# Two stores per token tile issued by ScalarE in place of SyncE, in a two-layer fp32 kernel

## The chip, the cores and the metric

The kernel runs on one core of a Trainium2 chip. The metric is the device time of one execution in microseconds, the median of several runs. Before the change it is 719.97 us (3 runs, 719.19 to 720.18).

## The reference

What is computed is two rounds of the same pair of residual blocks on x of 2048 tokens by 576 features:

```python
x = x + _A_ref(_layernorm(x), A_wqkv, A_wo)          # linear attention, 32 heads of 18
x = x + _B_ref(_layernorm(x), B_w_q, B_k1, B_k2, B_u, B_v)   # product-key experts, top 1 per head
```

Block A projects to q, k and v, applies phi(t) = elu(t) + 1 + 1e-6 to q and k, sums k times v over all tokens into one state per head, and divides q times state by q times the sum of k. Block B scores 64 experts per head, takes the best one, and adds gelu(x . u[e]) v[e].

## The kernel before

The 2048 tokens are 16 tiles of 128. A tile passes through named pieces of code, each a Python generator that is run up to its next `yield`. `front_T` (`fT`) turns the normalized tile so that features lie on partitions, and splits it into two float32r operands: `thif`, written by ScalarE (line 117), and `tlof`, the remainder, written by VectorE (line 118). `front_k`, `front_v` and `front_q` multiply them by the weights on TensorE (`ppk`, `ppv`, `ppq`, line 258); `front_state` adds the tile into the state (`kva`). For the second half of layer A, `num` divides (`o`), `oT` turns `o` into `thio` and `tloo`, `O` multiplies by the folded output weights (`ppo`, line 483) and adds the residual on VectorE (`x`, line 473). Block B is `bT`/`S` (scores, `kva` or `pps`, line 525), `gel`, `sel` (ten small VectorE operations that end in `cg`, line 590), `cT` (`ptc`, `chi`, `clo`) and `po` (line 609, residual again line 473).

A layer norm after a residual is a relay: VectorE's `x` with its sum, POOL's `mb` or `mf` (line 187), ScalarE's `junk` with a squared sum (line 188), three POOL instructions (`rsb` or `rsf`, 193 to 195), and ScalarE's `yb` or `yf` (line 205).

Most tiles of layer 0's second half and of layer 1's front are not turned on TensorE but by VectorE and memory (`moved`): VectorE transposes 32 by 32 squares (`ro`, `rb`, `rf`, line 229), one DMA stores 320 KB (`y_do`, `y_db`, `y_df`, line 231), and four DMAs of 80 KB load it back (`go`, `gb`, `gf`, line 237). The next reader is ScalarE's split at line 117.

Layer 1's q is not computed in the front. For tiles 0 to 12, `front_keep` (lines 330 to 334) stores `thif` and `tlof` of layer 1, 320 KB each, to `hl_d`; `late_load` (lines 340 and 341) loads them when the state is complete, from 499 us on.

The order of the work is written out by hand, in strings that `play` reads: `keep1.5` stands for `front_keep` of layer 1, tile 5. Within `in_order(*ALL)` the instructions of TensorE, ScalarE, VectorE and POOL stand exactly in that order. SyncE is not among them: its queue, which issues every DMA before the change, is ordered by the framework's scheduler. The middle part of the program (about 290 to 435 us) is one string of two tiles played four times, with other pieces before and after it. The framework gives the DMAs eight completion semaphores in turn; a DMA waits until the last DMA with its semaphore has landed.

```python
with in_order(*ALL):
    for s in range(5, 13, 2):
        play("""bT0.0 num0.2 ... ld0.3 k1.-3 O0.1 ... keep1.-2 v1.-2 po0.-1 ... keep1.-1 st1.-2 ...""", s)
```

Of the kernel before, what the change touches and what calls it, by code (L numbers as in the profile page):

```python
# [11 lines left out]
F32 = mybir.dt.float32  # L12
# [52 lines left out]
def network(ctx, tc, x_in, wqkv, wo, wq_t, k_t, u_t, v2, c_mask, c_mask4, c_ident, c_code, c_code1, c_scale, c_shift, out):  # L65
    nc = tc.nc
# [44 lines left out]
    hl_d = [dr.tile([P, 2, NB, P], F32, name=f"hl_d{t}") for t in range(NT)]  # L111
# [218 lines left out]
    def front_keep(l, t):  # L330

        hi, lo = tt["f", l, t]
        nc.sync.dma_start(hl_d[t][:, 0], hi.bitcast(F32))
        nc.sync.dma_start(hl_d[t][:, 1], lo.bitcast(F32))

    def late_load(l, t):

# [405 lines left out]

    bc = object()
    keep, rl, lq, ldx, ldq = front_keep, late_load, late_q, back_x, back_pq
    fl, ln, lv, sv = first_load, first_ln, load_vu, split_vu
    k, v, q, fT, st = front_k, front_v, front_q, front_T, front_state
# [210 lines left out]
```

## Time and profile before

| | |
|---|---|
| median of 3 runs | 719.97 us |
| the profiled execution, its own time | 720.89 us |
| its span (first to last instruction) | 719.1 us |
| mean granted TensorE clock | 0.997 |
| TensorE, VectorE, ScalarE, POOL busy | 698.8, 474.0, 320.9, 202.7 us |
| DMA bytes | 107 MB, all by SyncE's queue but for instruction loads |

Times in the views are microseconds from the start of the span. A row of the timeline has start, duration, engine (SPq is SyncE's queue, PEld TensorE's weight load), line, operation, tiles, shapes and count; in brackets stands the idle time of the engine just before, and what ended it. Rows of equal instructions are merged. Tile numbers are left out there; they follow from the order.

### The profile page before, as it was taken

Reading aid. Unit: us, or ns where it says so; the run is one execution under the profiler, and the core shown is the slowest. Engines: PE = TensorE matmul, PEld = TensorE weight load, DVE = VectorE, ACT = ScalarE, POOL = GpSimd, SP = SyncE. Lnnn points to the kernel's source line nnn. Section 1 sums busy time; section 2 is a strip of 40 time slices with the busy share of each in tenths; the row PEclk is TensorE's granted clock in tenths of the full one; section 3 lists DMA queues with packets and bytes.
Section 4 is the critical chain, followed back from the end, with each engine's and each line's share of the span. In section 5 each row is a group of like instructions: output and inputs, shape, how many; then the busy total and the mean of one; then the engine's idle time right before and its main releaser. Section 6 shows DMA issues by size and latency. Waiting matters only on the chain. (4 is left out here: it accounts for less than half of the span.)

```text
span 719.1 us, 14715 instructions
## 1 busy us (share of the span) xinstructions
PE 698.8 (97%) x5464; PEld 649.9 (90%) x5464; DVE 474.0 (66%) x1031; ACT 320.9 (45%) x658; POOL 202.7 (28%) x543
## 2 busy tenths in 40 slices
PE   8999999999999999999999999999999999999995
PEld 6999989999998999899898989899899999899984
DVE  5533343435437877687787878552647798988996
ACT  4522422342224456455555554644543534444443
POOL 2211000111004533344343433210323244433431
PEclk9999999999999999999999999999999999999998
DMA  8847777774312322476767665423632324111101
GB/s 252 274 159 249 262 237 260 253 216 137 112 33 67 100 103 102 147 232 199 238 219 234 205 198 172 138 61 121 170 106 83 112 71 134 51 67 51 51 17 66
DMA packets 82711, 107.17 MB, mean 149 GB/s; under 512 B 8976, under 2 KB 47376, under 8 KB 82640
## 3 DMA queue, kind: packets, MB, share of 16 engines
q1 hardware_dynamic: 82640, 106.24, 46.7%
q8 instruction: 43, 0.70, 0.4%
q14 instruction: 28, 0.23, 0.1%
HBM read 68.88 MB, written 37.32 MB: 148 GB/s over the span
## 5 line engine op out<-in xcount | busy, mean ns | idle before, releaser
L483 PE MATMUL ppo<-ohi,thio 126*128 126x252 f32 (+1 forms) x320 | 50.6, 300 | 3.9 <-ACT thio L117 3.9
L483 PEld LDWEIGHTS ppo<-ohi,thio 126*128 126x128 f32 (+1 forms) x320 | 44.9, 189 | 5.8 <-ACT thio L117 4.9
L188 ACT ACTIVATE junk<-x,mb 128x576 bf16<-128x576 f32 x32 | 24.8, 775 | 49.0 <-POOL mb L187 43.0
L205 ACT ACTIVATE yb<-x,rsb 128x640 f32<-128x640 f32 x32 | 29.5, 921 | 35.7 <-POOL rsb L195 35.7
L258 PE MATMUL ppk<-whi,thif 128*128 128x252 f32 (+1 forms) x300 | 45.2, 297 | 0.1
L258 PE MATMUL ppv<-whi,thif 128*128 128x252 f32 (+1 forms) x300 | 44.7, 295 | 0.1
L179 POOL TENSOR_SCALAR rsf<-mvf 128x1 f32<-128x1 f32 x16 | 3.4, 211 | 146.9 <-DVE mvf L176 146.8
L453 POOL TENSOR_TENSOR o<-pq,zb 128x576 f32<-128x576 f32 x19 | 27.3, 1439 | 60.9 <-ACT zb L399 57.4
L258 PE MATMUL ppv<-whi,tlof 128*128 128x252 f32 (+1 forms) x300 | 43.9, 293 | 0.0
L258 PE MATMUL ppk<-whi,tlof 128*128 128x252 f32 (+1 forms) x300 | 43.9, 293 | 0.0
L258 PEld LDWEIGHTS ppk<-whi,thif 128*128 128x128 f32 x300 | 40.9, 188 | 3.1 <-issue 2.9
L258 PEld LDWEIGHTS ppv<-whi,thif 128*128 128x128 f32 x300 | 41.3, 188 | 1.1 <-issue 0.4
L258 PEld LDWEIGHTS ppk<-whi,tlof 128*128 128x128 f32 x300 | 41.2, 188 | 0.0
L258 PEld LDWEIGHTS ppv<-whi,tlof 128*128 128x128 f32 x300 | 41.2, 188 | 0.0
L483 PE MATMUL ppo<-olo,thio 126*128 126x252 f32 (+1 forms) x256 | 39.6, 293 | 0.0
L258 PE MATMUL ppq<-whi 128*128 128x252 f32 (+1 forms) x260 | 39.5, 299 | 0.0
L483 PE MATMUL ppo<-ohi,tloo 126*128 126x252 f32 (+1 forms) x256 | 39.5, 293 | 0.0
L277 DVE TENSOR_SCALAR ek<-ek 128x576 f32<-128x576 f32 x16 | 7.4, 460 | 46.2 <-ACT ek L276 46.2
L258 PEld LDWEIGHTS ppq<-whi 128*128 128x128 f32 x260 | 36.0, 189 | 0.6 <-DVE eq L287 0.3
L483 PEld LDWEIGHTS ppo<-olo,thio 126*128 126x128 f32 x256 | 36.2, 188 | 0.0
L258 PE MATMUL ppk<-wlo,thif 128*128 128x252 f32 x240 | 36.1, 293 | 0.0
L258 PE MATMUL ppv<-wlo,thif 128*128 128x252 f32 x240 | 36.1, 293 | 0.0
(205 smaller groups left out, 1781.5 us busy)
## 6 DMA issues: line engine op xcount, KB each, us to landing
fold<-in_wq_t SPq DMA_DIRECT2D x64, 288.0 KB, 4.2
whi<-hl_d SPq DMA_DIRECT2D x26, 320.0 KB, 4.4
y_df<-rf SPq DMA_DIRECT2D x23, 320.0 KB, 3.0
gf<-y_df SPq DMA_DIRECT2D x92, 80.0 KB, 2.1
pq_d<-eq SPq DMA_DIRECT2D x19, 288.0 KB, 2.2
pq<-pq_d SPq DMA_DIRECT2D x19, 288.0 KB
xf<-in_x SPq DMA_DIRECT2D x16, 288.0 KB, 2.7
x<-in_x SPq DMA_DIRECT2D x16, 288.0 KB, 2.7
```

Source lines behind the costliest of these rows:

```text
L179: nc.gpsimd.tensor_scalar(rs[:, 0:1], mv[:, 1:2], EPS_LN, 1.0, op0=ALU.add, op1=ALU.mult)
L188: nc.scalar.activation(junk, xt, AF.Square, bias=m[:, 0:1], accum_out=m[:, 1:2])
L205: nc.scalar.activation(y, x2, AF.Identity, scale=rs[:, 0:1], bias=rs[:, 1:2])
L258: nc.tensor.matmul(o[:, at:at + c1 - c0], tt[a == "lo"][:, b, :], wb[:, cols + c0:cols + c1], start=(i == 0), stop=(i == len(todo) - 1))
L277: nc.vector.tensor_scalar(e, e, 1.0, EPS, op0=ALU.min, op1=ALU.add)
L453: nc.gpsimd.tensor_tensor(o[:, :D], pq, zb, op=ALU.mult)
L483: nc.tensor.matmul(p[:, at:at + c1 - c0], hl[a][:r, b], w[:r, c0:c1], start=(i == 0), stop=(i == len(todo) - 1))
```

## The change

The two stores of `front_keep` are issued by ScalarE's queue. With that they become ScalarE instructions, and `in_order` holds them at their place in the string.

```diff
     def front_keep(l, t):
 
         hi, lo = tt["f", l, t]
-        nc.sync.dma_start(hl_d[t][:, 0], hi.bitcast(F32))
-        nc.sync.dma_start(hl_d[t][:, 1], lo.bitcast(F32))
+        nc.scalar.dma_start(hl_d[t][:, 0], hi.bitcast(F32))
+        nc.scalar.dma_start(hl_d[t][:, 1], lo.bitcast(F32))
```

TensorE's and VectorE's rows stay as they were; ScalarE has 26 rows more and SyncE 26 fewer.

ScalarE, at tile 4 of layer 1 (the first of the even tiles 4, 6, 8, 10 of the repeated string). `hl_d_92` is tile 4's store, `thif_4` the operand just split, `junk,mb_7` the layer norm of tile 7 of layer 0:

```order
 L117 ACTIVATE thib_6_4135<-gb_6_4130 128x640
 L117 ACTIVATE thif_4_4157<-gf_4_4152 128x640
+L333 DMA hl_d_92<-thif_4_4157 128x640
+L334 DMA hl_d_92<-tlof_4_4158 128x640
 L188 ACTIVATE junk,mb_7_4244<-x_7_4209,mb_7_4244 128x576
 L117 ACTIVATE chi_5_4165<-ptc_5_4163 128x128
```

Both stores now stand between the split of `thif_4` and the square sum of tile 7; the second waits for VectorE's `tlof_4`.

ScalarE, at tile 5 (the odd tiles 3, 5, 7, 9), where `yf_6` is the end of another layer norm:

```order
 L205 ACTIVATE yb_8_4498<-x_8_4461,rsb_8_4494 128x640
 L188 ACTIVATE junk,mf_6_4500<-x_6_4489,mf_6_4500 128x576
+L333 DMA hl_d_93<-thif_5_4469 128x640
+L334 DMA hl_d_93<-tlof_5_4470 128x640
 L205 ACTIVATE yf_6_4538<-x_6_4489,rsf_6_4534 128x640
 L539 ACTIVATE g_7_4547<-s_7_4459 128x64
```

Here they stand between a square sum and the normalization that waits for POOL.

SyncE's queue at the same place, with `go_9` the four loads behind `y_do_9`:

```order
 L231 DMA y_do_9_4473<-ro_9_4471 128x640
-L333 DMA hl_d_93<-thif_5_4469 128x640
-L334 DMA hl_d_93<-tlof_5_4470 128x640
 L237 DMA go_9_4607<-y_do_9_4473 32x4x160
 L617 DMA x_d_142<-x_6_4489 128x576
-L237 DMA go_9_4607<-y_do_9_4473 32x4x160
+L237 DMA go_9_4607<-y_do_9_4473 32x4x160 x3
 L231 DMA y_db_8_4595<-rb_8_4593 128x640
-L237 DMA go_9_4607<-y_do_9_4473 32x4x160 x2
 L231 DMA y_df_6_4620<-rf_6_4618 128x640
```

The stores are gone, and the last two of the four loads stand ahead of `y_db_8` instead of behind it.

## Prediction

> **What bounds the kernel now.** I read the page first, then TensorE's timeline of the stretch that holds the stores, then the waits of that stretch, and from there back along the engines that TensorE waited for.
>
> ```profile
> PE 698.8 (97%) x5464; PEld 649.9 (90%) x5464; DVE 474.0 (66%) x1031; ACT 320.9 (45%) x658; POOL 202.7 (28%) x543
> L334 SPq DMA_DIRECT2D hl_d<-tlof x13: 319/320/434, 263.8 to 456.5; - x13
> ```
>
> TensorE is busy for 97% of the span, so a change that leaves it alone can save at most its 20 us of idle time, and costs only where it makes TensorE wait. The second store of each tile (from the rows of `hl_d`: count, duration min/median/max in ns, first and last start) comes between 263.8 and 456.5 us. TensorE's timeline there has few gaps:
>
> ```profile
> 350.41 0.33 PE L512 MATMUL ptc<-ident,cg 128*128 128x128 f32 x1
> 351.57 1.59 PE L483 MATMUL ppo<-ohi,thio 126*128 126x252 f32 x10 [0.83 <-ACT thio L117]
> 384.33 1.59 PE L483 MATMUL ppo<-ohi,thio 126*128 126x252 f32 x10 [0.89 <-ACT thio L117]
> 417.05 1.59 PE L483 MATMUL ppo<-ohi,thio 126*128 126x252 f32 x10 [0.83 <-ACT thio L117]
> 437.70 0.51 PE L609 MATMUL po<-vmix,chi 128*128 128x252 f32 x2 [0.87 <-DVE ek L287]
> ```
>
> The repeated string takes 32.7 us for two tiles, and in each turn TensorE waits 0.83 to 0.89 us for ScalarE's `thio` of the odd tile. So each turn is bound by a loop through the other engines, not by TensorE. Its last links are these, of SyncE's queue and of ScalarE:
>
> ```profile
> 340.70 0.32 SPq L231 DMA_DIRECT2D y_do<-ro  x1
> 341.75 0.32 SPq L333 DMA_DIRECT2D hl_d<-thif  x1
> 342.61 0.32 SPq L334 DMA_DIRECT2D hl_d<-tlof  x1
> 344.24 0.32 SPq L237 DMA_DIRECT2D go<-y_do  x1
> 344.65 0.41 SPq L617 DMA_DIRECT2D x_d<-x  x1
> 345.11 0.42 SPq L237 DMA_DIRECT2D go<-y_do  x1
> 345.69 0.34 SPq L231 DMA_DIRECT2D y_db<-rb  x1
> 346.08 2.00 SPq L237 DMA_DIRECT2D go<-y_do  x2
> 350.78 0.74 ACT L117 ACTIVATE thio<-go 128x640 fp32r<-128x640 f32 x1 [2.38 <-DMA go<-y_do]
> ```
>
> ScalarE idles 2.38 us for the last `go`. The first `go` waits for the landing of `y_do`, not for the stores of `hl_d`; the last two stand behind `y_db`, whose data VectorE has only just made.
>
> **The stores on the even tiles: a wait in ScalarE.** The loop's earlier links, ScalarE first, then VectorE:
>
> ```profile
> 323.05 0.74 ACT L117 ACTIVATE thif<-gf 128x640 fp32r<-128x640 f32 x1 [1.45 <-DMA gf<-y_df]
> 324.43 0.78 ACT L188 ACTIVATE junk<-x,mb 128x576 bf16<-128x576 f32 x1 [0.63 <-POOL mb L187]
> 324.26 0.82 DVE L118 TENSOR_TENSOR tlof<-gf,thif 128x640 fp32r<-128x640 f32 x1
> 327.46 0.85 DVE L229 STREAM_TRANSPOSE rb<-yb 128x640 f32<-128x640 f32 x1 [1.68 <-ACT yb L205]
> 336.70 0.76 DVE L287 SCALAR_TENSOR_TENSOR ek<-ek,ppk 128x576 f32<-128x576 f32 x1 [0.38 <-ACT ek L286]
> 349.98 0.29 DVE L590 TENSOR_TENSOR cg<-g,c 128x128 f32<-128x128 f32 x1
> ```
>
> Before, `junk` starts at 324.43. Now it stands behind the second store, which waits until `tlof` is written at 324.26 + 0.82 = 325.08. The first store's issue fits ahead of that. How soon a store follows its `tlof`, SyncE showed a tile earlier:
>
> ```profile
> 310.23 0.82 DVE L118 TENSOR_TENSOR tlof<-gf,thif 128x640 fp32r<-128x640 f32 x1 [0.91 <-ACT thif L117]
> 311.08 0.32 SPq L334 DMA_DIRECT2D hl_d<-tlof  x1
> ```
>
> `tlof` ends at 311.05 and the issue starts 0.03 us later; by the row of line 334 an issue takes 0.32 to 0.43 us. No row shows a DMA issued by ScalarE; its cost lies between nothing and SyncE's longest issue of these tiles, 1.49 us:
>
> ```profile
> L237 SPq DMA_DIRECT2D go<-y_do x32: 318/444/1487, 312.3 to 424.9; - x32
> ```
>
> I take 0.38, the middle of the store's own rows. So `junk` moves by 0.65 + 0.03 + 0.38 = **1.06 us**, and with it everything queued behind: `chi`, POOL's `rsb`, `yb`, and VectorE's `rb`, which waited for `yb` already. VectorE then runs without a gap until `ek` at 336.70, whose 0.38 us wait takes up that much. From there the shift is 1.06 - 0.38 = 0.68 us, at `ro` (and so `y_do`) and at `cg`.
>
> Two chains then end at the same TensorE rows. By `cg`: 349.98 + 0.29 + 0.68 = 350.95, so `ptc` moves from 350.41 to 350.95 and `ppo` could start 0.33 later, at 351.3; that is 0.26 us earlier than 351.57, if `thio` is there. By `go`: 0.68 us later than 351.57, less what SyncE's shorter queue gives.
>
> **What SyncE's shorter queue gives.** The last two `go` no longer wait for `y_db`: with 0.43 us each behind the second they start at 345.54 and 345.97 (before, 346.08 and about 0.5 later), so some 0.55 us sooner. They also no longer lie behind the 320 KB of `y_db`. At the best rate of the stretch from 300 to 440 us (40 slices of it), 338 GB/s, that is 0.95 us:
>
> ```profile
> GB/s 241 135 207 332 237 197 236 313 240 120 133 164 333 245 173 173 273 338 124 143 168 321 266 153 160 262 301 209 167 96 260 298 260 107 181 297 251 101 129 99
> ```
>
> Against this stand the stores themselves. Before they moved at 342 to 345 us, while `go` had to wait for `y_do` anyway. Now ScalarE issues them behind `junk` of `mf`:
>
> ```profile
> 344.79 0.19 ACT L188 ACTIVATION_READ_ACCUMULATOR junk<-x,mf 128x1 f32 x1
> 346.19 0.92 ACT L205 ACTIVATE yf<-x,rsf 128x640 f32<-128x640 f32 x1 [1.21 <-POOL rsf L195]
> ```
>
> The two issues, 0.76 us, fit in the 1.21 us in which `yf` waits for POOL, so ScalarE loses nothing on odd tiles. But 640 KB, 1.9 us at 338 GB/s, now run beside the very loads that TensorE waits for. The gain is 0.55 + 0.95 less 0 to 1.9, that is -0.4 to 1.5 us; I take 0.3, near the low end, because the stores start within a microsecond of the loads. The Trainium skill (DMA: Bandwidth & Descriptors, section "Issuing engines are not separate DMA queues") says that DMAs of all engines interleave on the same 16 DMA engines, and that issuing from another engine saves only the sequencer's time; by it the gain would be the 0.55 alone less the sharing. The trace of before has one queue and can't show it.
>
> So a turn changes by 0.68 - 0.3 = **+0.4 us**, with ends of -0.26 (the `cg` chain) and +1.1. There are three such turns (351.57, 384.33, 417.05): **+1.2 us**. The turn before them has no even store behind it yet, and I count nothing.
>
> **The last even tile.** Tile 10's stores stand at 422.6, and its loop ends elsewhere, at TensorE's 437.70:
>
> ```profile
> 422.45 0.82 DVE L118 TENSOR_TENSOR tlof<-gf,thif 128x640 fp32r<-128x640 f32 x1
> 422.61 0.78 ACT L188 ACTIVATE junk<-x,mb 128x576 bf16<-128x576 f32 x1 [0.59 <-POOL mb L187]
> 425.65 0.85 DVE L229 STREAM_TRANSPOSE rb<-yb 128x640 f32<-128x640 f32 x1 [1.68 <-ACT yb L205]
> 435.74 0.35 DVE L460 RECIPROCAL r<-den 128x32 f32<-128x32 f32 x1 [0.41 <-POOL den L457]
> 437.47 0.28 DVE L118 TENSOR_TENSOR clo<-ptc,chi 128x128 fp32r<-128x128 f32 x1
> ```
>
> The shift is 423.27 + 0.03 + 0.38 - 422.61 = 1.07 us. VectorE has no gap between 425.65 and `clo` but the 0.41 us for POOL's `den`, which follows VectorE's own and moves along. TensorE, which waited 0.87 us here, waits **1.07 us** more.
>
> **The other stores.** Tile 11's stores stand late in the string, between the third folded weight and the second late q:
>
> ```profile
> 514.97 0.65 ACT L423 ACTIVATE ohi<-m 126x576 fp32r<-126x576 f32 x1
> 515.95 0.65 ACT L284 ACTIVATE eq<-ppq 128x576 f32<-128x576 f32 x1 [0.33 <-PE ppq L258]
> 518.58 1.35 PEld L258 LDWEIGHTS ppq<-whi 128*128 128x128 f32 x10 [0.30 <-DVE eq L287]
> ```
>
> 0.76 us of issue less the 0.33 us of idle delay `eq`, on whose end the next `ppq` waits already: **+0.43 us** (0 to 2.6). Tile 0's stores stand ahead of `junk` at 278.74, those of tiles 1 and 2 ahead of 292.91, tile 12's ahead of 458.18:
>
> ```profile
> 278.74 0.78 ACT L188 ACTIVATE junk<-x,mf 128x576 bf16<-128x576 f32 x1 [1.41 <-POOL mf L187]
> 292.91 0.78 ACT L188 ACTIVATE junk<-x,mb 128x576 bf16<-128x576 f32 x1 [3.86 <-POOL mb L187]
> 458.18 0.60 ACT L530 ACTIVATE s<-kva 128x512 f32<-128x512 f32 x1 [0.93 <-PE kva L525]
> ```
>
> The idle times of 1.41, 3.86 and 0.93 us hold 0.76, 1.52 and 0.76; I count nothing. If an issue took 0.6 us, tile 12 would cost 0.3.
>
> **Sum.** 1.2 + 1.07 + 0.43 = +2.7 us on the profiled execution's 720.89 (span 719.1 and 1.8 around it). The median of the runs is 0.9 below that execution, so the forecast is 719.97 + 2.7 = **722.7 us**.
>
> **Rivals.** *The loads gain more.* If the stores hardly disturb the `go` loads (a gain of 1.0 or more), each turn is set by the `cg` chain: 3 x -0.26 + 1.07 + 0.43 = +0.7, 720.7 us. For it speaks that ScalarE waits only for the last `go`, which loses both `y_db` and its issue; against it that 640 KB fall on it.
>
> *Faster.* If a waiting store didn't hold back ScalarE's next instruction, nothing would shift: the turns would lose their TensorE waits, -0.83, -0.89 and -0.83, with nothing against it, 719.97 - 2.55 = 717.4 us. It decides from a shift of `junk` below 0.3 us. Against it stands SyncE's queue, where a store that waits does hold up those behind it:
>
> ```profile
> SPq L333 <- ACT thif L117: 22.8, 12, 7.2
> ```
>
> It is 22.8 us in 12 waits there, while the idle row before `junk` shows only 0.63 us to hide in.
>
> *A dearer issue.* ScalarE's even store falls among SyncE's four `go` (0.44 us median each), its odd stores among those at 345.1 to 346.5. If one issue has to wait for the other queue's, a store costs 0.38 + 0.44 = 0.82. Then the even shift grows by 0.44 (four times, 1.8 us), the odd pair takes 1.64 in a 1.21 us gap (0.43 at four tiles, of which three sit in the bound turns, 1.3 us), and tile 11 costs 0.9 more: 2.7 + 4.0 = +6.7, 726.7 us. The Trainium skill (Perfetto Trace Analysis, section on the HWDGE DMA instruction) says that the descriptor generator is shared by two sequencers and locked for each DMA, and that the profiled issue includes the wait for the lock. In the trace of before only one queue issues, so it shows nothing on it; the 1.49 us issue is a wait of some kind.
>
> *The change doesn't do what it says.* The order of the built program excludes that: 26 rows moved.
>
> **How the numbers follow.** Chances: forecast 0.5, the larger gain 0.22, the dearer issue 0.18, faster 0.1. A measurement of this kernel tells 0.2%, 1.4 us, from no change: below 718.5 is faster, above 721.4 slower. The forecast's own spread by the ends of its terms is 720.7 (turns at -0.26) to 724.8 (turns at +1.1), so about a tenth of its chance lies inside 0.2%; with the larger gain that makes 0.27 for the same. The range runs from 718.9 to 727.5: it takes in the larger gain and the dearer issue, and leaves out the faster case and an issue at 1.49 us.
>
> **What would show it.** In the changed profile: ScalarE rows at line 334 whose issue ends about 0.4 us after `tlof`, `junk` near 325.5 without a wait for POOL; VectorE's wait for `yb` near 2.7 instead of 1.68 us; TensorE's wait at `po` near 1.9 instead of 0.87 us; in the turns, waits for `cg` at `ptc` where there were none, and a shorter ScalarE wait for `go`. I am wrong if line 334's rows are longer than 0.6 us, if ScalarE's wait for `go` grows beyond 2.38 us, or if `junk` hasn't moved.

## The result, and the profile after

The changed kernel takes 726.21 us (median of 4 runs, 725.53 to 727.22) against 720.08 us of the kernel before beside it (4 runs, 719.19 to 720.76): ratio 1.0082, 95% interval 1.0069 to 1.0096, so 6.1 us slower where 2.7 were forecast. Its profiled span is 723.7 us against 719.1, 4.6 longer; the profiled execution of before was itself 0.8 us above its median, that of the changed kernel 0.7 below.

From the page of the changed kernel, TensorE's busy time and the new second DMA queue (packets, MB, share of the 16 engines' time), which carries the 26 stores:

```profile
PE 702.0 (97%) x5464; PEld 650.5 (90%) x5464; DVE 474.3 (66%) x1031; ACT 320.4 (44%) x658; POOL 202.7 (28%) x543
q10 hardware_dynamic: 3744, 8.52, 3.3%
```

From the changed kernel's rows of line 333 and line 334, the price of an issue (duration min/median/max in ns, first and last start):

```profile
L333 ACTq DMA_DIRECT2D hl_d<-thif x13: 326/326/420, 274.7 to 518.5; - x13
L334 ACTq DMA_DIRECT2D hl_d<-tlof x13: 326/444/648, 275.1 to 518.8; - x13
```

The median issue takes ScalarE's queue 0.33 us for `thif` and 0.44 for `tlof`, where SyncE's took 0.32; the even tiles' stores, for which ScalarE waits, take 0.33. The dearer issue isn't the reason.

From TensorE's timeline of the changed kernel, the rows at which the pieces of the repeated string begin and end:

```profile
318.31 1.59 PE L483 MATMUL ppo<-ohi,thio 126*128 126x252 f32 x10
...
352.09 1.57 PE L483 MATMUL ppo<-ohi,thio 126*128 126x252 f32 x10 [0.56 <-ACT thio L117]
356.67 1.44 PE L525 MATMUL kva<-shi,thib 128*128 128x512 f32 x5 [0.66 <-ACT thib L117]
...
386.34 1.57 PE L483 MATMUL ppo<-ohi,thio 126*128 126x252 f32 x10 [0.91 <-ACT thio L117]
390.62 1.43 PE L525 MATMUL kva<-shi,thib 128*128 128x512 f32 x5 [0.36 <-ACT thib L117]
...
420.49 1.57 PE L483 MATMUL ppo<-ohi,thio 126*128 126x252 f32 x10 [0.96 <-ACT thio L117]
...
442.89 0.50 PE L609 MATMUL po<-vmix,chi 128*128 128x252 f32 x2 [1.29 <-DVE ek L287]
```

The wait for the odd tile's `thio` is about as long as before (0.56 against 0.83 at 352.09, 0.91 against 0.89 at 386.34, 0.96 against 0.83 at 420.49), and there are new ones for `thib`. The three turns take 352.09 - 318.31 = 33.78, then 34.25 and 34.15 us; before they took 32.68, 32.76 and 32.72. So they lose 1.1, 1.5 and 1.4 us instead of 0.4 each. The piece from 420.49 to `po` takes 22.40 us instead of 20.65, 1.75 more instead of 1.07. The first of these rows stands 0.58 us earlier than before, so `po` is 5.19 us later, and from there to the end nothing is added.

What ScalarE did at the even store of tile 4 (ScalarE's timeline of the changed kernel; ACTq is its DMA queue):

```profile
323.71 0.74 ACT L117 ACTIVATE thif<-gf 128x640 fp32r<-128x640 f32 x1 [1.16 <-DMA gf<-y_df]
324.48 0.33 ACTq L333 DMA_DIRECT2D hl_d<-thif  x1
325.34 0.33 ACTq L334 DMA_DIRECT2D hl_d<-tlof  x1
325.71 0.78 ACT L188 ACTIVATE junk<-x,mb 128x576 bf16<-128x576 f32 x1 [1.26 <-DVE tlof L118]
```

And VectorE at the same place:

```profile
324.48 0.83 DVE L118 TENSOR_TENSOR tlof<-gf,thif 128x640 fp32r<-128x640 f32 x1 [0.69 <-ACT thif L117]
326.77 0.29 DVE L118 TENSOR_TENSOR clo<-ptc,chi 128x128 fp32r<-128x128 f32 x1 [1.47 <-ACT chi L117]
328.75 0.84 DVE L229 STREAM_TRANSPOSE rb<-yb 128x640 f32<-128x640 f32 x1 [1.68 <-ACT yb L205]
```

`tlof` ends at 325.31, the issue starts 0.03 us later and `junk` 0.40 us after `tlof`, where 0.41 was forecast. But `tlof` is late too. Counted from the odd tile's `ppo` (318.31 in this run, 318.89 before), it starts at 6.17 us instead of 5.37. Together `junk` is 1.86 us late: 1.06 of the wait and issue, 0.80 of something else.

That something is in SyncE's queue of the changed kernel. The loads of the next turn show it:

```profile
341.52 0.32 SPq L231 DMA_DIRECT2D y_do<-ro  x1
344.88 0.32 SPq L237 DMA_DIRECT2D go<-y_do  x1
...
345.76 2.16 SPq L237 DMA_DIRECT2D go<-y_do  x3
347.96 1.35 SPq L231 DMA_DIRECT2D y_db<-rb  x1
...
352.13 1.92 SPq L237 DMA_DIRECT2D gb<-y_db  x4
```

and in ScalarE's timeline of the changed kernel beside it:

```profile
344.12 0.92 ACT L205 ACTIVATE yb<-x,rsb 128x640 f32<-128x640 f32 x1 [0.78 <-POOL rsb L195]
344.52 0.33 ACTq L333 DMA_DIRECT2D hl_d<-thif  x1
344.88 0.45 ACTq L334 DMA_DIRECT2D hl_d<-tlof  x1
344.95 0.76 ACT L188 ACTIVATE junk<-x,mf 128x576 bf16<-128x576 f32 x1
...
351.31 0.74 ACT L117 ACTIVATE thio<-go 128x640 fp32r<-128x640 f32 x1 [2.07 <-DMA go<-y_do]
355.88 0.74 ACT L117 ACTIVATE thib<-gb 128x640 fp32r<-128x640 f32 x1 [2.16 <-DMA gb<-y_db]
357.61 0.74 ACT L117 ACTIVATE thif<-gf 128x640 fp32r<-128x640 f32 x1 [0.99 <-DMA gf<-y_df]
```

For comparison, the rows of the kernel before that its prediction didn't need (the `ppo` of the turn ahead, and ScalarE's splits of this turn):

```profile
318.89 1.56 PE L483 MATMUL ppo<-ohi,thio 126*128 126x252 f32 x10
353.91 0.74 ACT L117 ACTIVATE thib<-gb 128x640 fp32r<-128x640 f32 x1 [0.72 <-DMA gb<-y_db]
355.96 0.74 ACT L117 ACTIVATE thif<-gf 128x640 fp32r<-128x640 f32 x1 [1.31 <-DMA gf<-y_df]
```

`y_db` now stands behind all four `go`: it is issued 6.44 us after `y_do` (347.96 - 341.52) instead of 4.99. The two odd stores go out at 344.52 and 344.88, the second at the very moment of the first `go`. `thib` starts 3.79 us after its turn's `ppo` instead of 2.34, `thif` 5.52 instead of 4.39.

### The profile page after: what moved, and what is told of

The parts are those of the page before. It is cut to its first block, busy times and chain, and to the rows that moved or that the text cites. A ratio compares the mean times of both kernels' runs of the same rounds, so it can differ in the third digit from the quotient of the medians.

```text
span 723.7 us, 14699 instructions
## 1 busy us (share of the span) xinstructions
PE 702.0 (97%) x5464; PEld 650.5 (90%) x5464; DVE 474.3 (66%) x1031; ACT 320.4 (44%) x658; POOL 202.7 (28%) x543
## 5 line engine op out<-in xcount | busy, mean ns | idle before, releaser
L483 PEld LDWEIGHTS ppo<-ohi,tloo 126*128 126x128 f32 x256 | 36.0, 188 | 0.0
```

The lines of the kernel that those rows point to most:

```text
L483: nc.tensor.matmul(p[:, at:at + c1 - c0], hl[a][:r, b], w[:r, c0:c1], start=(i == 0), stop=(i == len(todo) - 1))
```

## The experiments

Three theories were set against each other. **W**: ScalarE's even store, which waits for `tlof`, makes all of the loss. **T**: the odd stores do, by their bytes beside `go` and `y_db`. **M**: both, and the late loads are dear mainly because a store now waits for what they feed. The changed kernel is called "after" below. Times are against the kernel before on the same chip, from the ratio of the runs and a median of 722.3 us there; these chips are not the one of the first result.

| run | even stores | odd stores | ratio (95%) | us |
|---|---|---|---|---|
| after, again | ScalarE, wait | ScalarE, beside `go` | 1.0064 (1.0048 to 1.0080) | +4.6 |
| e1 | SyncE | ScalarE, beside `go` | 1.0008 (0.9991 to 1.0024) | +0.6 |
| e2 | ScalarE, wait | SyncE | 1.0032 (1.0013 to 1.0052) | +2.3 |
| e3 | ScalarE, late | ScalarE, beside `go` | 1.0008 (0.9995 to 1.0021) | +0.6 |
| e4 | ScalarE, wait | ScalarE, earlier | 1.0026 (1.0013 to 1.0040) | +1.9 |
| e5 | ScalarE, late | ScalarE, earlier | 0.9969 (0.9954 to 0.9984) | -2.2 |
| e5, again | as e5 | as e5 | 0.9972 (0.9961 to 0.9984) | -2.0 |
| e6 | `thif` ScalarE, `tlof` SyncE | the same | 0.9998 (0.9987 to 1.0009) | -0.1 |
| e7 | SyncE, and a wait (new tile) | SyncE | 1.0114 (1.0090 to 1.0138) | +8.2 |
| e8 | SyncE, and a wait | SyncE | 1.0036 (1.0022 to 1.0050) | +2.6 |
| e9 | as e5, `y_db` ahead of two `go` | as e5 | 0.9998 (0.9982 to 1.0014) | -0.1 |
| e10 | as after, `y_db` ahead of two `go` | as after | 1.0069 (1.0055 to 1.0082) | +5.0 |

**e1, the even stores back on SyncE.**

```diff
-        nc.scalar.dma_start(hl_d[t][:, 0], hi.bitcast(F32))
-        nc.scalar.dma_start(hl_d[t][:, 1], lo.bitcast(F32))
+        (nc.sync if t in (4, 6, 8, 10) else nc.scalar).dma_start(hl_d[t][:, 0], hi.bitcast(F32))
+        (nc.sync if t in (4, 6, 8, 10) else nc.scalar).dma_start(hl_d[t][:, 1], lo.bitcast(F32))
```

> The changed kernel, with the stores of tiles 4, 6, 8 and 10 issued by SyncE again; those of the odd tiles and of 0, 1, 2, 11, 12 stay with ScalarE. Of the changed kernel's +6.1 us, theory W (ScalarE's even store waits for tlof and holds back junk and all behind it) says that the even stores make all of it: 720.1 to 720.5 us here, junk back on POOL's mb, turns of 32.7 us. Theory T (the odd tiles' stores run beside go and y_db, so gb, gf and their splits come late) says that the odd stores make it: 725 to 726.5 us here, turns of 34.2 us. Theory M (mixed: the late loads cost by themselves little, because junk doesn't need tlof, and become dear only by the store that waits for tlof): thif still comes about 1.1 us late in the turn, of which POOL's 0.6 us gap ahead of junk and VectorE's 0.38 us wait take nearly all; 720.3 to 721.3 us.

Measured +0.6 us (-0.7 to 1.7). T falls: with the odd stores alone moved, little is lost against the kernel before. M's number fits, its reason only half. From ScalarE's timeline of e1:

```profile
388.96 0.74 ACT L117 ACTIVATE thib<-gb 128x640 fp32r<-128x640 f32 x1 [1.92 <-DMA gb<-y_db]
390.84 0.74 ACT L117 ACTIVATE thif<-gf 128x640 fp32r<-128x640 f32 x1 [1.14 <-DMA gf<-y_df]
391.48 0.76 ACT L188 ACTIVATE junk<-x,mb 128x576 bf16<-128x576 f32 x1
```

and from its TensorE timeline:

```profile
385.42 1.59 PE L483 MATMUL ppo<-ohi,thio 126*128 126x252 f32 x10 [0.39 <-ACT thio L117]
389.75 1.44 PE L525 MATMUL kva<-shi,thib 128*128 128x512 f32 x5 [0.39 <-ACT thib L117]
```

The loads are as late as in after (`thib` 3.54 us behind `ppo`; 3.49 in after's turn at 386.34), and `junk` follows `thif` at once, without POOL's gap: that slack took part of it, as M says. But TensorE also stalls for `thib`, which M had left out.

**e2, the odd stores back on SyncE** (the same edit with tiles 3, 5, 7 and 9).

> The changed kernel, with the stores of tiles 3, 5, 7 and 9 issued by SyncE again; those of the even tiles stay with ScalarE. Theory W: the even wait makes all of it, 725 to 726.5 us, turns of 34.2 us. Theory T: without the odd stores beside the loads nothing is left, 720.1 to 721 us. Theory M: only the 1.06 us of the wait and the issue is left, less VectorE's 0.38 us: 0.68 in each of three turns and 1.07 at tile 10, so 723.0 us (722.5 to 723.6), turns of 33.4 us, tlof back at its time of before in the turn (5.4 us after ppo), junk 1.06 us late.

Measured +2.3 us (0.9 to 3.8): W, which wanted 5 to 6.5, falls, T too; M's +3.0 is inside the interval.

**e3, the even stores later.** `keep1.-1` moves to the end of the repeated string.

```diff
-            bT0.1 fT1.-1 S0.1 keep1.-1 st1.-2 O0.2 cT0.0 O0.2 po0.0 oT0.3 S0.1
+            bT0.1 fT1.-1 S0.1 st1.-2 O0.2 cT0.0 O0.2 po0.0 oT0.3 S0.1 keep1.-1
```

> The changed kernel with all stores on ScalarE, but the even tile's store stands at the end of the repeated string, some 5 us later, when tlof has long been written. It waits for nothing there. Theory W: 720.1 to 721 us. Theory T: the odd stores are as in the changed kernel, 725 to 726.5 us. Theory M: as with the even stores on SyncE, 720.3 to 721.5 us, if the later 640 KB don't run into other loads; turns of 32.7 to 33.0 us, and no idle time of ScalarE for tlof.

Measured +0.6 us (-0.4 to 1.5), like e1. So the even stores cost no more as ScalarE's than as SyncE's when their data is old; what they cost in after is the wait. The next two runs test the wait by itself.

**e7 and e8, the wait alone.** Both are the kernel before with one added ScalarE instruction on tiles 4, 6, 8 and 10, a copy of one element per partition of `tlof`. In e7 it writes a new tile of four bytes per partition, allocated among the constants; in e8 it writes `junk`'s tile. The diff is that of e8.

```diff
-        nc.sync.dma_start(hl_d[t][:, 1], lo.bitcast(F32))
+        nc.sync.dma_start(hl_d[t][:, 1], lo.bitcast(F32)); t in (4, 6, 8, 10) and nc.scalar.activation(junk[:, :1], lo[:, 0, :1].bitcast(F32), AF.Copy)
```

> The kernel before, all stores on SyncE, with one added ScalarE instruction at the place of the store on tiles 4, 6, 8 and 10: a copy of one element per partition of tlof. It is the wait alone, no DMA is moved. With a copy of about 0.2 us junk moves by 0.65 + 0.03 + 0.2 = 0.9 us. Theory W, if the wait makes all of the +6.1: 724.5 to 726 us. Theory T: 720.1 to 720.6 us. Theory M: 0.9 - 0.38 = 0.5 us in each of three turns and 0.9 at tile 10: 722.5 us (722 to 723).

Measured +8.2 us, which no theory allowed. TensorE's timelines show that most of it isn't the wait. Busy times of e7 from 100 to 200 us, long ahead of the first probe (sum, TensorE with its count of matmuls, weight loads, VectorE, ScalarE, POOL, then the granted clock, the DMA share and GB/s):

```profile
100.00:200.00 100.00, 100.00 (x901) 94.92 (x900) 42.28 (x85) 32.56 (x76) 8.51 (x24) 1.00 0.63 199
```

One group of ten matmuls in that stretch, first in before, then in e7:

```profile
152.49 1.46 PE L258 MATMUL ppk<-whi,thif 128*128 128x252 f32 x10
155.01 1.49 PE L258 MATMUL ppk<-whi,thif 128*128 128x252 f32 x10
```

TensorE is fully busy at a granted clock of 1.00, and these matmuls take 2% longer; over the whole run TensorE is busy for 711.3 us instead of 698.8. Not all matmuls are slower: the `kva` group of 40 at 60 us takes 1.43 us in both, so it isn't the clock. In e8, which has the copy and no new tile, the ten take 1.46 us as before. The new tile comes ahead of later buffers in the same memory; what about it slows the matmuls these runs don't show. e7 says nothing on the wait, and e8 took its place.

> The wait alone once more, now without a new tile: the kernel before, all stores on SyncE, with one ScalarE copy of one element per partition of tlof (into the square sum's scratch tile, which it overwrites anyway) at the place of the store on tiles 4, 6, 8 and 10. No buffer's address differs from the kernel before. Theory M: junk about 0.9 us later, less VectorE's 0.38, in each of three turns and 0.9 at tile 10: +2.5 us (+1.8 to +3). Theory W: +4.5 to +6. Theory T: 0 to +0.4. If the +8.6 us of the first try came from the wait and not from the tile that it added, +8 again.

Measured +2.6 us (1.6 to 3.6), M's number. ScalarE's rows in e8, the probe and `junk` behind it:

```profile
325.78 0.21 ACT L334 ACTIVATE junk<-tlof 128x1 bf16<-128x1 f32 x1 [1.20 <-DVE tlof L118]
326.08 0.78 ACT L188 ACTIVATE junk<-x,mb 128x576 bf16<-128x576 f32 x1
```

`junk` starts 6.54 us behind its turn's `ppo` there instead of 5.54. So the wait costs on its own, without one DMA moved. W as the whole cause falls.

**After, again**, to have it beside the others.

> The changed kernel once more, beside the runs that follow. The first four experiments ran on another chip than the changed kernel: there the odd stores alone cost 0.6 us and the even ones alone 2.3 (each with 1.2 us either way), 2.9 together, against 6.1 of the changed kernel. If the two costs simply add and only the chip differs, +2.9 to +4.5 us here. If each makes the other dearer (theory M: late loads meet a store that waits), +5.5 to +6.5 again.

Measured +4.6 us (3.5 to 5.8), between the two cases; the chips differ (before takes 722.3 there, 2.2 us more than in the first result, after 727.1, 0.9 more).

**e4, the odd stores earlier.** `keep1.-2` moves ahead of one `O` and one `po`, so ahead of `yb` in ScalarE's order.

```diff
-            num0.3 po0.-1 S0.0 O0.1 po0.-1 keep1.-2 v1.-2 po0.-1 sel0.0 ...
+            num0.3 po0.-1 S0.0 keep1.-2 O0.1 po0.-1 v1.-2 po0.-1 sel0.0 ...
```

> The changed kernel with the odd tiles' stores some 1 us earlier in ScalarE's order, ahead of yb: they are issued while y_do is on its way, as SyncE did it, and no longer at the moment in which the go loads start. The even stores wait for tlof as in the changed kernel. Theory M: what is left is the even wait, as with the odd stores on SyncE, +2.3 to +3.1 us, turns of about 33.4 us, y_db landing as early after y_do as before. Theory W: +5.5 to +6.5. If the shorter time between y_do and its loads is not what made the loads late (but that y_db stands behind all four go), +5 to +6.

Measured +1.9 us (0.9 to 2.9) by the ratio; the medians, 725.27 and 722.31, are 3.0 apart, since its runs fall into two groups (722.4 to 723.5 and 725.1 to 725.9). Either way 1.9 to 2.7 us less than after: where the odd stores fall matters. ScalarE's and TensorE's rows in e4:

```profile
384.87 0.74 ACT L117 ACTIVATE thio<-go 128x640 fp32r<-128x640 f32 x1 [1.17 <-DMA go<-y_do]
385.76 1.56 PE L483 MATMUL ppo<-ohi,thio 126*128 126x252 f32 x10
389.97 1.44 PE L525 MATMUL kva<-shi,thib 128*128 128x512 f32 x5 [0.30 <-ACT thib L117]
```

`ppo` no longer waits for `thio`, here and in the next turn (in the turn ahead it waits 0.36 us): `thio` starts 8.87 us behind `y_do`, in after's same turn 10.12. The wait for `thib` stays, against the expectation, so it isn't the stores' moment that makes `y_db` late.

**e5, both moved**, the edits of e3 and e4 together.

> Both moved: the odd stores as early as in the run before, the even stores at the end of the string where tlof is long written, all on ScalarE. Theory M: nothing of either cost is left, -0.5 to +0.7 us, turns of 32.5 to 32.9 us; below 0 if SyncE's shorter queue gives the go loads anything. If the collision remains (the stores anywhere near y_do or go cost), +0.6 to +2.

Measured -2.2 us (-3.3 to -1.2), below what theory M allowed (-0.5 to +0.7). It was run once more on another chip:

> The kernel with both stores placed once more, beside the run with y_db first: -1.5 to -2.9 us against the kernel before, as measured (ratio 0.9969).

Measured -2.0 us (-2.8 to -1.2). This version is faster than both kernels, and 0.3% faster than the one before. ScalarE's rows of one turn of e5:

```profile
375.68 0.33 ACTq L333 DMA_DIRECT2D hl_d<-thif  x1
376.27 0.33 ACTq L334 DMA_DIRECT2D hl_d<-tlof  x1
...
383.37 0.74 ACT L117 ACTIVATE thio<-go 128x640 fp32r<-128x640 f32 x1 [1.30 <-DMA go<-y_do]
387.60 0.74 ACT L117 ACTIVATE thib<-gb 128x640 fp32r<-128x640 f32 x1 [1.82 <-DMA gb<-y_db]
```

and SyncE's:

```profile
377.45 0.32 SPq L237 DMA_DIRECT2D go<-y_do  x1
...
378.32 1.46 SPq L237 DMA_DIRECT2D go<-y_do  x3
379.83 0.43 SPq L231 DMA_DIRECT2D y_db<-rb  x1
```

ScalarE's wait of the same turn in the kernel before:

```profile
383.55 0.74 ACT L117 ACTIVATE thio<-go 128x640 fp32r<-128x640 f32 x1 [2.44 <-DMA go<-y_do]
```

The stores start 1.8 and 1.2 us ahead of `go`, and ScalarE waits 1.30 us for `go` instead of 2.44. `thib` is still late, with `y_db` behind four `go`.

The four runs with all stores on ScalarE make a square: taking away the even wait gives 4.0 us with the odd stores beside `go` (1.0064 to 1.0008) and 4.1 with them early (1.0026 to 0.9969); moving the odd stores gives 2.7 and 2.8. By these ratios the two add, each difference with some 1.5 us either way (e3 is of another chip; with the medians in place of e4's ratio its 4.1 would read 4.7, and its 2.7 would read 1.9). What is left when both are gone is a gain of 2 us. That is also why e1 and e3 read only +0.6: in them the odd stores' 2.8 stands against this gain.

**e10 and e9, SyncE's old order.** For `y_do` of tiles 7, 9 and 11 and j > 1, an order-only dependency on the `y_db` store recorded last (`rows[-1]`) puts `y_db` ahead of the last two `go` again, on after (e10) and on e5 (e9).

```diff
         for j in range(4):
-            nc.sync.dma_start(g[32 * j:32 * j + 32], ...)
+            nc.sync.dma_start(g[32 * j:32 * j + 32], ...); n in ("o0_7", "o0_9", "o0_11") and j > 1 and tc.add_manual_dep(nc.cur_bb.bb.instructions[-1], rows[-1].name, ...)
```

> The changed kernel with one thing of SyncE's old order put back: in the three turns y_db stands ahead of the last two of the four go loads, not behind them. Stores as in the changed kernel. Theory O (the late thib comes of y_db's place in the queue, which the shorter queue let slip behind go): y_db about 1 us earlier, thib and thif back near 2.3 and 4.3 us after ppo, TensorE's waits for thib gone; only the even wait is left, and the go loads now pay for y_db and the odd stores: +2.3 to +3.5 us against the kernel before. Theory T (the odd stores' bytes beside go and y_db make it): nothing changes, +4.5 to +6.

Measured +5.0 us (4.0 to 5.9): theory O, that the order makes the loss, falls. What it said of the splits is right all the same. ScalarE's rows in e10:

```profile
388.82 0.74 ACT L117 ACTIVATE thio<-go 128x640 fp32r<-128x640 f32 x1 [2.85 <-DMA y_df<-rf]
391.89 0.74 ACT L117 ACTIVATE thib<-gb 128x640 fp32r<-128x640 f32 x1 [0.66 <-DMA gb<-y_db]
393.85 0.74 ACT L117 ACTIVATE thif<-gf 128x640 fp32r<-128x640 f32 x1 [1.22 <-DMA gf<-y_df]
```

and TensorE's:

```profile
389.61 1.59 PE L483 MATMUL ppo<-ohi,thio 126*128 126x252 f32 x10 [1.34 <-ACT thio L117]
```

`thib` and `thif` stand 2.28 and 4.24 us behind `ppo`, as before the change, TensorE's wait for `thib` in this turn is gone, and its wait for `thio` is 1.34 us instead of 0.91. So here the order of the queue decides which load pays: in the first of these turns `thio` starts 11.33 us behind `y_do` (9.13 in after), and `ppo` comes at 322.11 instead of 318.31. The last turn, whose `y_do` the edit leaves out, still has the late `thib` (3.60 us behind `ppo`).

> Both stores placed (odd early, even at the end of the string) and y_db ahead of the last two go loads. Theory O: TensorE's waits for thib (0.3 to 0.9 us a turn with both placed) go; the go loads come 0.5 to 1 us later, against a slack of at least that in two of three turns: -2.5 to -3.5 us against the kernel before, 0.3 to 1 us below the run with both placed. If the go loads decide instead (y_db's 320 KB beside them), waits for thio come back, 0.5 to 0.9 us a turn, and it is -1.5 to 0.

Measured -0.1 us (-1.3 to 1.0): with the stores out of the way the old order isn't better, by the ratio it is 1.9 us worse than e5 beside it, by the medians (721.14 and 720.39) 0.8. Its TensorE rows show the wait for `thio` again (0.81 us at 384.72), as the second half of its expectation had it; theory O's -2.5 to -3.5 falls here too.

**e6, only `tlof`'s store on SyncE.**

```diff
-        nc.scalar.dma_start(hl_d[t][:, 1], lo.bitcast(F32))
+        (nc.sync if 3 <= t <= 10 else nc.scalar).dma_start(hl_d[t][:, 1], lo.bitcast(F32))
```

> The changed kernel with only the first store (thif) on ScalarE and the second (tlof) on SyncE, for tiles 3 to 10. ScalarE has written thif itself, so it waits for nothing. Theory M: the even wait's share is gone; junk is late by one issue (0.35 us) where POOL's 0.6 us gap hides it. What is left depends on the odd thif store beside go (half the bytes) and on the order that SyncE gets: 0 to +1.5 us. Theory W: 0 to +0.5. Theory T with half the bytes: +2 to +3.

Measured -0.1 us (-0.9 to 0.7). ScalarE's rows in e6 at an even tile:

```profile
357.83 0.33 ACTq L333 DMA_DIRECT2D hl_d<-thif  x1
358.20 0.78 ACT L188 ACTIVATE junk<-x,mb 128x576 bf16<-128x576 f32 x1 [0.40 <-POOL mb L187]
```

The store of ScalarE's own result waits for nothing and fits in POOL's gap. Half of theory T's cost, +2 to +3, isn't there.

## Why the prediction was right in direction and too small

**The issue.** Forecast 0.38 us, measured 0.33 for the even tiles' stores, and 0.44 as the median of line 334. The dearer issue asked for 0.82 and falls, though its 726.7 us came nearest to the measured 726.2; that is luck. The odd `tlof` store took 0.45 us beside SyncE's `go`, but those of tiles 0 and 11, also right behind their `thif` stores, took 0.44 (at 275.10 and 518.83) while SyncE issued nothing. So these rows show no wait for the lock of which the Trainium skill speaks (Perfetto Trace Analysis, section on the HWDGE DMA instruction).

**The even wait.** Forecast: `junk` 1.06 us later, and VectorE's wait for `yb` at 2.7. The wait and issue cost 1.06, but `junk` is 1.86 us late in its turn, with the 0.80 of `tlof`. VectorE's wait is longer by 1.06, but one instruction earlier, at `clo` (1.47 us instead of 0.42), while `rb` keeps its 1.68. The `ek` wait of 0.38 is gone, as forecast. One gap ahead of `ek` was overlooked, 0.19 us for the even tile's `thio` at 334.07; it moves along with ScalarE and is still there (335.36). Three turns of 0.68 and 1.07 for tile 10 made 3.1 us; e8, with a 0.21 us copy in place of the issue, cost 2.6, against 2.5 expected. In the changed kernel the same wait is worth 4.0 by the runs' times, 1.4 more, which the spread of both figures could make alone. The rows speak for a real difference: in e8 `y_do` comes 22.1 to 22.4 us behind the `ppo` of the turn ahead, in the changed kernel 23.2 to 23.3, before 21.8. I put it down to `tlof`, which comes 0.80 us later in the changed kernel: in e1 the late loads met POOL's gap ahead of `junk`, here they meet a store that waits for them.

**What SyncE's shorter queue gives.** This is the step that failed. A turn was to win 0.3 us here (-0.4 to 1.5), all of it at `go`, and at `go` the forecast was near:

- `thio` starts 9.79, 10.12 and 10.19 us behind `y_do` in the three turns, before 10.08, 10.14 and 10.08: 0.3, 0.0 and -0.1 us won.
- Its two parts were about right too. With the odd stores out of the way (e4) `thio` comes 9.58, 8.87 and 8.32 us behind `y_do`, so 0.5 to 1.8 us are won where 1.5 was counted, and the stores beside `go` take 0.2 to 1.9 of it back where I allowed 1.2.

The loss stands ahead of `y_do`. It comes 23.21, 23.34 and 23.17 us behind the `ppo` of the turn ahead instead of 21.81 to 21.85, so 1.3 to 1.5 us late where 0.68 was forecast: `junk`'s 1.86 less some 0.4 of VectorE's slack. What was put at nothing is the 0.80 of `tlof` in it. I counted that `go` no longer waits for `y_db`, and not that `y_db` now waits for `go`: 6.44 us behind `y_do` instead of 4.99. The order of the changed program showed it. Over the profiles the queue's order sorts the turns: where `y_db` stands behind all four `go` (after, e1, e4, e5, the last turns of e9 and e10), `thib` starts 3.2 to 4.5 us behind `ppo`; where it stands ahead of one or two of them (before, e2, e6, e8, the other turns of e9 and e10), 1.5 to 2.7.

The odd stores also start earlier than forecast. I put them behind `junk` of `mf`; ScalarE's queue issues them while `yb` still runs, ahead of `junk`, just when `go` starts.

By the square the odd stores cost 2.7 to 2.8 us at the place where the change puts them. With both stores placed, a gain of 2.0 to 2.2 us is left, larger than the 0.9 that the three turns were to win. 4.0 + 2.8 - 2.2 = 4.6 is the changed kernel there, taken apart; the three are differences between the same runs, so that they add up to 4.6 proves nothing. The Trainium skill (DMA: Bandwidth & Descriptors, section "Issuing engines are not separate DMA queues") has the DMAs of all issuing engines interleave on the same 16 DMA engines; the trace agrees, since stores on ScalarE's queue made SyncE's loads late (`thio` 10.12 us behind `y_do` in after, 8.87 in e4, where the stores go out earlier).

**The rest.** Tile 11's 0.43 us did not come: ScalarE's wait for `ppq` behind it is 0.33 us as before. The two stores were issued at 518.47 and 518.83, beside earlier arithmetic of ScalarE, and not in the gap at 520.77 where I had put them. TensorE's wait at `po` is 1.29 us, not 1.9; other waits of that piece, for `thib` (0.42) and `thio` (0.33), make up for it. From `po` to the end the run loses nothing (5.19 us late at `po`, 4.6 at the end). Tiles 0, 1, 2 and 12 cost nothing, as forecast. Waits for `cg` at `ptc` did not appear in the turns; TensorE waited there for `thio` and `thib`. Of the signs of being wrong two came: ScalarE's wait for `go` was 2.42 and 2.49 us in the last two turns, above 2.38 (though before had 2.44 in one of them), and one of the 13 rows of line 334 took 0.65 us, at 289.07, the last of four stores in a row.

**The rivals.** "Loads gain more" asked for +0.7 us and fell with the `go` loads, which gained 0.3 us in one turn and nothing in the others. "Faster" asked for -2.6; a waiting store does hold back ScalarE.

**Left open.** Where e5's 2 us come from isn't settled: its turns in the profile (32.76 and 32.20 us) are hardly shorter than those of the profile of before, which ran on another chip. Nor is it settled why the changed kernel lost 6.1 us on the first chip and 4.6 on the second.

## What to carry to other kernels

A DMA that moves to a computing engine's queue is an instruction of that engine: it waits for its data there, and everything behind it waits too, so place it where its data is old, or move only the store of the engine's own result. Look then at the queue that it leaves: what moved up, and what now stands behind it. A slack that hides a late load today may be the cover of the new wait; test both parts alone and together.

## What the runs showed of the hardware

ScalarE's queue issued a store at 344.52 us while its `yb` ran until 345.04 and its `junk`, which stands ahead of the store in the order, started at 344.95. So a DMA that waits for nothing passes arithmetic that stands ahead of it. One that waits holds up arithmetic behind it: at tile 4 the next `junk`, which doesn't read `tlof`, started 0.40 us after `tlof` ended.

A second store issued 0.36 or 0.39 us behind the first took 0.44 us (tiles 11 and 0 of the changed kernel), one issued 0.86 us behind it 0.33 (tile 4).

With a new tile of four bytes per partition in a place ahead of others (e7), the same ten matmuls took 1.49 us instead of 1.46, at a granted clock of 1.00 in both.
